# Moving a finished chunk's split and logits, and the next batch's key chunk, to other places in the order of an attention and mixture-of-experts kernel

## The chip, the cores and the metric

The kernel runs on one core of a Trainium2 chip, as one program and one launch. The metric is the time on the device in microseconds (us): the median of three runs, 1411.36 us, with 1410.93 and 1411.73 as the lowest and the highest.

## What is computed

Two steps follow each other. The first is an attention without softmax over 8 batches of 2496 rows: scores of z with itself, squared after a ReLU, times v, and the result times u. The second sends each of the 19968 rows to one of 8 experts and computes an expert's two-layer network for its 80 rows of highest gate weight alone; all other rows of the output are zero.

```python
def _attn_ref(u, v, z):
    scale = 1.0 / S
    scores = scale * np.matmul(z, z.transpose(0, 2, 1))
    attn = np.maximum(scores, 0.0) ** 2
    out = np.matmul(attn, v)
    return u * out

def _moe_ref(x, w_gate, w1, w2, capacity):
    logits = x @ w_gate
    expert_idx = np.argmax(logits, axis=1)
    ...
    for e in range(E):
        ...
            keep = np.argpartition(-gw, capacity)[:capacity]
        h = np.maximum(x[tok_idx] @ w1[e], 0.0)
        out[tok_idx] = gate_w[tok_idx, None] * (h @ w2[e])
```

## The kernel before, in words

The 2496 rows of a batch are padded to 20 tiles of 128. Queries are taken in 5 chunks of 4 tiles (the last chunk has 448 columns, not 512), keys in 10 pairs of tiles. A step is one (batch b, chunk qc, pair r); the 400 steps are one list, and the loop over it writes out the order of each engine's work by hand: under `manual_schedule` PE, ACT, DVE and SP run their instructions in the order in which the loop issues them. Each of these engines takes its instructions strictly one after the other, so an instruction that waits holds everything behind it.

A step has two sides. `scores` (line 312) prepares a pair that is used two steps later (`LOOK` is 2). For a pair not yet seen PE makes two score tiles `s` (lines 326, 327, two matmuls each), ACT applies ReLU and square (lines 330, 331), and the result `a` is split into a rounded part `ah` (a cast on ACT or DVE, lines 105 and 107) and the remainder `al` (a subtraction on DVE, line 54). Since the scores are symmetric, pairs of key chunks before qc are not computed again: DVE transposes them when they are first made (`mirror`, line 265), a DMA stores them to DRAM (`y`), another reads them back (`blk`), and `mirrored` (line 299) casts `ah` on ACT (line 310) and subtracts `al` on DVE. `attend` (line 341) is then PE's main work: for each of the two key tiles and two halves of the output three matmuls of 512 columns, v's rounded part with `ah`, its remainder with `ah`, and its rounded part with `al` (lines 358 to 360; lines 362 and 363 for the padded last tile). The pools bound how far the engines can be apart: three `s` tiles, two `a`, three `ah` and three `al`.

When a chunk's ten pairs are done, its result is finished during the next chunk's steps:

- `chunk_x` (line 380): DVE multiplies the accumulated tile by u into `xf`, two instructions at line 377, at the start of the next chunk's step r = 0, ahead of that step's `scores`.
- `chunk_hi`, `chunk_rest`, `chunk_mid`, `chunk_lo` (lines 386 to 400): x is split into three bf16 parts. ACT casts `xb<-xf` (line 388), DVE subtracts `xr` (line 54), ACT casts `xb<-xr` (line 396), DVE subtracts the third part.
- `chunk_store`, `chunk_store2`: SP issues two DMA transposes of `xf` (line 427) and a store (line 436).
- `chunk_logits`, `chunk_sum`: 24 small matmuls on PE (line 451) and a reduction on DVE (line 459) give the gate logits.

`finished` (line 714) says at which step r of the next chunk each of these is issued; `at_end` is the last batch's fourth chunk, which has steps of its own, with `gate_top` and `gate_near` (DVE work on the batch's logits, with one ACT exponential at line 483). The loop itself is at lines 770 to 822. The fourth chunk of a batch starts with the pairs 8 and 9 and goes on with 0 to 7.

The next batch's keys are loaded one chunk of 512 columns at a time: SP issues `load_z` (line 100) at r = 1, and `prep_zc` (line 109) splits it on DVE in two instructions (a cast at line 112 and a subtraction at line 54, together `zc`) at r = 9.

After the last batch, DVE and PE finish the last chunk's x and logits, rows are picked, gathered and sent through the experts' matmuls.

Of the kernel before, what the change touches and what calls it, by code (L numbers as in the profile page):

```python
# [25 lines left out]
def attn_moe_kernel(ctx, tc, zT, uT, v, wg, w1, w2, out, seq, cap):  # L26
# [341 lines left out]
    def chunk_tiles(b, qc):  # L368
        xf = xpool.tile([P, DC, CH], F32, tag="xf", name=f"xf_{b}_{qc}")

        xb = xpool.tile([P, 3, DC, CH], BF16, tag="xb", name=f"xb_{b}_{qc}")
        xr = xpool.tile([P, DC, CH], F32, tag="xr", name=f"xr_{b}_{qc}")
        nq = min(CH, seq - qc * CH)
        xt_t[b, qc] = [x[..., :nq] for x in (xf, xb, xr)]

    def x_full(b, qc, c, s):
        V.scalar_tensor_tensor(out=xt_t[b, qc][0][:, c, s], in0=acc_t[b, qc][c][:, s], scalar=CSQ,  # L377
                               in1=u_t[b, qc][:, c, s], op0=ALU.mult, op1=ALU.mult)

    def chunk_x(b, qc):  # L380
        s = slice(0, min(CH, seq - qc * CH))
        chunk_tiles(b, qc)
        for c in range(DC):
            x_full(b, qc, c, s)

    def chunk_hi(b, qc):
        xf, xb, _ = xt_t[b, qc]
        nc.scalar.copy(out=xb[:, 0], in_=xf)  # L388

    def chunk_rest(b, qc):  # L390
        xf, xb, xr = xt_t[b, qc]
        tt(xr, xf, xb[:, 0], ALU.subtract)

    def chunk_mid(b, qc):
        _, xb, xr = xt_t[b, qc]
        nc.scalar.copy(out=xb[:, 1], in_=xr)  # L396
# [317 lines left out]
    def finished(b, qc, r):  # L714

        at_end = b == B - 1 and qc == NQ - 2
        if r == 0:
            chunk_hi(b, qc)
        elif r == 1:
            chunk_rest(b, qc)  # L720
        if r == (3 if at_end else 1):
            chunk_store(b, qc)
        if r == (5 if at_end else 3):
            chunk_store2(b, qc)
        if r == 1 and at_end or r == 2 and not at_end:
            chunk_mid(b, qc)
        if r == (2 if at_end else 3):
            chunk_lo(b, qc)
        if r == (4 if at_end else 6):
            chunk_logits(b, qc)  # L730
            chunk_sum(b, qc)
        kb = b * BPB
        if b < B - 1 and qc == NQ - 1:
            if r == 7:
                gate_top(b, 0, NQ)
            elif r == 8:
                gate_sum(b, gate_near(b, 0), gp)
        elif qc == 0 and b > 0:
            part = kb - BPB, kb
            if r == 2:  # L740
                count(*part)
            elif r == 4:
                up_to(*part)
                blocks(ps_m, "m", gp, oh, *part)
        elif at_end:
            part = kb, kb + BPB - 2
            if r == 5:
                gate_top(b, 0, NQ - 1)
            elif r == 6:
                gate_near(b, 0)  # L750
            elif r == 8:
                count(*part)
                up_to(*part)
                half()
            elif r == 9:
                blocks(ps_m, "m", gp, oh, *part)

    with tc.manual_schedule(engines={ET.PE, ET.Activation, ET.DVE, ET.SP}):
        prep_zc(0, 0, raw0)
        prep_zd(0, 0, raw0)  # L760
        prep_v(0, 0, vraw0, V, V)
        prep_zc(0, 1, raw12[:, 0])
        scores(0, 0, 0)
        scores(0, 0, 2)
        warm(WARM0, ps_m, "m")
        v_raw[0, 1] = vraw1
        z_raw.update({(0, 2): raw12[:, 1], (0, 3): raw34[:, 0], (0, 4): raw34[:, 1]})
        constants()
        prev = None
        for i, (b, qc, r) in enumerate(steps):  # L770
            last = b == B - 1 and qc == NQ - 1
            now[0] = i
            if r == 0 and prev:
                chunk_x(*prev)
            if (b, qc) == (0, 0) and r in (0, 2, 4):
                prep_zc(0, r // 2 + 2, z_raw.pop((0, r // 2 + 2)))
            if i + LOOK < len(steps):
                nb, nqc, nr = steps[i + LOOK]
                scores(nb, nqc, 2 * pairs_of[nqc][nr])
            if b == 0 and qc == 0:  # L780
                if r % 2 == 0 and r < 8:
                    g = r // 2 + 1
                    prep_v(0, g, v_raw.pop((0, g)), nc.scalar, V)
                    if g + 1 < NQ:
                        v_raw[0, g + 1] = load_v(0, g + 1)
                if r == 8:
                    constants_v()
            p = pairs_of[qc][r]
            for k in (2 * p, 2 * p + 1):
                if not last or k < NT - 3:  # L790
                    attend(b, qc, k)
            if prev:
                finished(*prev, r)

            nb, nqc = (b, qc + 1) if qc + 1 < NQ else (b + 1, 0)
            if r == 2:
                prep_u(b, qc)
            if b + 1 < B:
                if r == 1:
                    z_raw[b + 1, qc] = load_z(b + 1, qc)  # L800
                if r == 9:
                    prep_zc(b + 1, qc, z_raw.pop((b + 1, qc)))
                if qc == NQ - 2 and r in (2, 4):
                    g = r // 2 - 1
                    v_raw[b + 1, g] = load_v(b + 1, g)
                if qc == NQ - 1:
                    g = (r - 1) // 2 if r < 9 else 4
                    if r in (2, 4, 6, 8, 9):
                        prep_v(b + 1, g, v_raw.pop((b + 1, g)), nc.scalar, V)
                        if g + 2 < NQ:  # L810
                            v_raw[b + 1, g + 2] = load_v(b + 1, g + 2)
            if nb < B and r == 1:
                prep_zd(nb, nqc)
            if r == 5 and b < B - 1:
                zero_out(b * NQ + qc, B * NQ)
            if r == 8 and b == 0:
                zero_out((B - 1) * NQ + qc, B * NQ)
            if b == B - 1 and qc >= NQ - 3:
                weights_ahead(qc, r)
            mirror_back()  # L820
            mirror_out()
            if r == NP - 1:
                prev = b, qc

        chunk_tiles(*prev)
        for kk, c in ((3, 0), (2, 0), (3, 1), (1, 0), (2, 1), (1, 1)):
            attend(*prev, NT - kk, [c])
            if kk == 1:
                chunk_x_last(*prev, c)
        chunk_store(*prev)  # L830
        chunk_logits_last(*prev)
        gate_top(b, NQ - 1, NQ)
        chunk_store2(*prev)
        kb = B * BPB
        count_last(kb - 2, kb)
        blocks(ps_s, "s", gp, oh, kb - 2, kb)
        ranks()
# [562 lines left out]
```

## Time and profile before

| what | value |
|---|---|
| median of 3 runs | 1411.36 us |
| lowest to highest | 1410.93 to 1411.73 us |
| the profiled execution | 1410.26 us |
| its span, first to last instruction | 1408.5 us |
| PE (matmuls) busy | 1373.3 us, 97% |
| PE's weight loads busy | 1139.7 us, 81% |
| DVE busy | 1063.8 us, 76% |
| ACT busy | 1002.6 us, 71% |
| POOL busy | 35.4 us, 3% |
| DMA queues, share of 16 engines | 79.6% and 0.4% |

The page tells of one profiled execution. The span runs from its first instruction to its last. The busy time of an engine is the time in which it has an instruction in work; the busy shares are means over stages that differ: seven batches that are alike, a last batch, and some 90 us of expert work behind it. In a timeline each row is one instruction (or several alike in a row, marked x2, x8) with its start and its length in us; brackets give the idle time of the engine just before it and what ended that idle time. A matmul's length is longer than its distance from the next, since matmuls overlap in the array; the distance of two starts tells the pace.

### The profile page before, as it was taken

The page shows a single profiled execution, that of the slowest core. Times are in us where ns is not written, and L with a number is a line of the kernel's source. Part 1 is how long each engine was busy: PE and PEld are TensorE (multiplying, and loading weights), DVE is VectorE, ACT ScalarE, POOL GpSimd, SP SyncE. Part 2 cuts the span into 40 slices and gives each one's busy share as a digit, 9 for nine tenths or more (in the row PEclk, how much of TensorE's full clock was granted, in tenths as well). Part 3 has the DMA queues.
Part 4 walks back from the last instruction along what each step waited for, and adds up shares of the span by engine and source line. Part 5 has one row for each costly group of instructions (what it writes and reads, how often), then busy time and mean ns, then how long its engine had stood idle before and what let it go on. Part 6 is the DMA issues. An engine that isn't in the chain of part 4 may idle for free. (4 is left out here: it accounts for less than half of the span.)

```text
span 1408.5 us, 19544 instructions
## 1 busy us (share of the span) xinstructions
PE 1373.3 (97%) x7086; PEld 1139.7 (81%) x7087; DVE 1063.8 (76%) x1517; ACT 1002.6 (71%) x1282; POOL 35.4 (3%) x56
## 2 busy tenths in 40 slices
PE   9999999999999999999999999999999999999777
PEld 7887888888887888878888888878888788888566
DVE  8876788667877678767886678776886678867864
ACT  8875777757777587757787577766877577876365
POOL 0000000000000000000000000000000000000152
PEclk9999999999999999999999999999999999999889
DMA  6899777995888966996789958889668967889673
GB/s 223 254 254 264 207 220 225 246 264 156 227 231 236 265 176 197 253 260 172 221 232 246 255 166 232 228 231 259 175 204 249 262 168 202 239 222 244 170 231 93
DMA packets 260070, 311.89 MB, mean 221 GB/s; under 512 B 96152, under 2 KB 188192, under 8 KB 249728
## 3 DMA queue, kind: packets, MB, share of 16 engines
q1 hardware_dynamic: 258752, 309.02, 79.6%
q0 software_dynamic: 1216, 1.56, 0.4%
q8 instruction: 57, 0.93, 0.3%
q14 instruction: 45, 0.37, 0.1%
HBM read 153.48 MB, written 126.37 MB: 199 GB/s over the span
## 5 line engine op out<-in xcount | busy, mean ns | idle before, releaser
L360 PE MATMUL acc<-al,vt 128*128 128x512 f32 (+1 forms) x1520 | 585.5, 385 | 8.3 <-DVE al L54 8.3
L359 PE MATMUL acc<-ah,vt 128*128 128x512 f32 (+1 forms) x1520 | 584.7, 385 | 0.0
L358 PE MATMUL acc<-ah,vt 128*128 128x512 f32 (+1 forms) x1520 | 584.4, 384 | 0.0
L54 DVE TENSOR_TENSOR al<-a,ah 128x1024 fp32r<-128x1024 f32 (+1 forms) x240 | 291.4, 1214 | 136.1 <-ACT ah L105 128.4
L330 ACT ACTIVATE a<-s 128x512 f32<-128x512 f32 (+1 forms) x480 | 258.3, 590 | 129.6 <-PE s L327 128.4
L360 PEld LDWEIGHTS acc<-al,vt 128*128 128x128 f32 x1520 | 285.3, 188 | 64.1 <-DVE al L54 12.3
L359 PEld LDWEIGHTS acc<-ah,vt 128*128 128x128 f32 x1520 | 285.2, 188 | 53.7 <-DVE vt L146 0.8
L358 PEld LDWEIGHTS acc<-ah,vt 128*128 128x128 f32 x1520 | 285.4, 188 | 52.9
L331 ACT ACTIVATE a<-a 128x1024 f32<-128x1024 f32 (+1 forms) x240 | 253.0, 1054 | 7.6
L54 DVE TENSOR_TENSOR al<-blk,ah 128x1024 fp32r<-128x1024 f32 x160 | 193.7, 1216 | 42.9 <-ACT ah L310 40.7
L310 ACT CAST ah<-blk 128x1024 fp32r<-128x1024 f32 x160 | 165.4, 1048 | 76.9 <-PE acc L359 54.9
L265 DVE STREAM_TRANSPOSE x<-a 128x512 f32<-128x512 f32 x320 | 207.6, 687 | 0.0
L327 PE MATMUL s<-zd,zc 128*128 128x512 f32 (+1 forms) x480 | 186.9, 389 | 0.0
L105 ACT CAST ah<-a 128x1024 fp32r<-128x1024 f32 x153 | 160.8, 1051 | 4.8
L107 DVE CAST ah<-a 128x1024 fp32r<-128x1024 f32 (+1 forms) x87 | 59.2, 680 | 111.1 <-ACT a L331 111.0
L326 PE MATMUL s<-zc,zc 128*128 128x512 f32 x320 | 128.8, 403 | 1.7 <-ACT a L330 1.7
L327 PEld LDWEIGHTS s<-zd,zc 128*128 128x128 f32 x480 | 90.4, 188 | 16.2 <-issue 0.5
L388 ACT CAST xb<-xf 128x1024 bf16<-128x1024 f32 (+1 forms) x39 | 40.1, 1028 | 83.4 <-DVE xf L377 83.4
L326 PEld LDWEIGHTS s<-zc,zc 128*128 128x128 f32 x320 | 60.1, 188 | 15.2 <-ACT a L330 4.3
L326 PE MATMUL s<-zc 128*128 128x512 f32 (+1 forms) x160 | 63.6, 397 | 0.0
L396 ACT CAST xb<-xr 128x1024 bf16<-128x1024 f32 (+1 forms) x39 | 40.0, 1024 | 28.2 <-DVE xr L54 27.7
L146 DVE TENSOR_TENSOR vt<-vraw,vt 128x1024 fp32r<-128x1024 f32 (+1 forms) x40 | 46.5, 1163 | 6.8 <-ACT vt L105 6.5
(171 smaller groups left out, 841.9 us busy)
## 6 DMA issues: line engine op xcount, KB each, us to landing
y<-x SPq DMA_DIRECT2D x80, 1024.0 KB
blk<-y SPq DMA_DIRECT2D x320, 256.0 KB
out<-idle SPq DMA_DIRECT2D x40, 512.0 KB
vraw<-v SPq DMA_DIRECT2D x32, 512.0 KB
ut<-uT SPq DMA_DIRECT2D x32, 512.0 KB
xs<-xq SPq DMA_DIRECT2D x32, 512.0 KB
wraw<-w SPq DMA_DIRECT2D x28, 512.0 KB
zd<-zc SPq DMA_DIRECT2D x78, 128.0 KB
```

Source lines behind the costliest of these rows:

```text
L54: V.tensor_tensor(out=o, in0=a, in1=b, op=op)
L105: eng.copy(out=o, in_=i)
L107: eng.tensor_copy(out=o, in_=i)
L265: V.transpose(out=x[:, :, :, t].rearrange("p n k s -> p k n s"), in_=a)
L310: nc.scalar.copy(out=natural(ah), in_=src)
L326: nc.tensor.matmul(s[:, :nq], zk, zc[:, :nq], start=True, stop=False)
L327: nc.tensor.matmul(s[:, :nq], zk, zd[:, :nq], start=False, stop=True)
L330: nc.scalar.activation(out=a[:, h, :nq], in_=s[:, :nq], func=AF.Relu)
L331: nc.scalar.activation(out=a[:, :, :nq], in_=a[:, :, :nq], func=AF.Square)
L358: nc.tensor.matmul(o, vt[:, t, 0, cs], ah, start=k == first, stop=False)
L359: nc.tensor.matmul(o, vt[:, t, 1, cs], ah, start=False, stop=False)
L360: nc.tensor.matmul(o, vt[:, t, 0, cs], al, start=False, stop=k == last)
```

## The change

Three things move, and nothing is added or removed.

1. `chunk_x` is issued behind step r = 0's `scores`, not ahead of it. Since the order on DVE is the order of issue, the remainder `al` of the pair that is used two steps later now stands ahead of the two x instructions.
2. `finished` issues the parts of the split a step later: `chunk_hi` at r = 1 for 0, `chunk_rest` at 2 for 1, `chunk_mid` at 3 for 2, `chunk_lo` at 4 for 3 (in the last batch's fourth chunk `chunk_mid` at 2 for 1, `chunk_lo` at 3 for 2). The store's steps stay. The logits stay at r = 6, and in the last batch's fourth chunk move from r = 4 to r = 5, with `gate_top` from 5 to 6 and `gate_near` from 6 to 7.
3. `prep_zc` for the next batch is issued at r = 5, not r = 9. Its load stays at r = 1.

```diff
@@ -714,19 +714,19 @@
     def finished(b, qc, r):
 
         at_end = b == B - 1 and qc == NQ - 2
-        if r == 0:
+        if r == 1:
             chunk_hi(b, qc)
-        elif r == 1:
+        elif r == 2:
             chunk_rest(b, qc)
         if r == (3 if at_end else 1):
             chunk_store(b, qc)
         if r == (5 if at_end else 3):
             chunk_store2(b, qc)
-        if r == 1 and at_end or r == 2 and not at_end:
+        if r == (2 if at_end else 3):
             chunk_mid(b, qc)
-        if r == (2 if at_end else 3):
+        if r == (3 if at_end else 4):
             chunk_lo(b, qc)
-        if r == (4 if at_end else 6):
+        if r == (5 if at_end else 6):
             chunk_logits(b, qc)
             chunk_sum(b, qc)
         kb = b * BPB
@@ -744,9 +744,9 @@
                 blocks(ps_m, "m", gp, oh, *part)
         elif at_end:
             part = kb, kb + BPB - 2
-            if r == 5:
+            if r == 6:
                 gate_top(b, 0, NQ - 1)
-            elif r == 6:
+            elif r == 7:
                 gate_near(b, 0)
             elif r == 8:
                 count(*part)
@@ -770,13 +770,13 @@
         for i, (b, qc, r) in enumerate(steps):
             last = b == B - 1 and qc == NQ - 1
             now[0] = i
-            if r == 0 and prev:
-                chunk_x(*prev)
             if (b, qc) == (0, 0) and r in (0, 2, 4):
                 prep_zc(0, r // 2 + 2, z_raw.pop((0, r // 2 + 2)))
             if i + LOOK < len(steps):
                 nb, nqc, nr = steps[i + LOOK]
                 scores(nb, nqc, 2 * pairs_of[nqc][nr])
+            if r == 0 and prev:
+                chunk_x(*prev)
             if b == 0 and qc == 0:
                 if r % 2 == 0 and r < 8:
                     g = r // 2 + 1
@@ -798,7 +798,7 @@
             if b + 1 < B:
                 if r == 1:
                     z_raw[b + 1, qc] = load_z(b + 1, qc)
-                if r == 9:
+                if r == 5:
                     prep_zc(b + 1, qc, z_raw.pop((b + 1, qc)))
                 if qc == NQ - 2 and r in (2, 4):
                     g = r // 2 - 1
```

How the rows stand on the engines, at three places. In these names the first numbers are the chunk and the key tile or part, the last one counts buffers.

DVE, batch 1, start of the fourth chunk (`al_3_0` is the remainder of the pair used at r = 2, `xf_2` the third chunk's x), before:

```order
L112 CAST zc_2_2729<-zraw_2469 128x512
L54 TENSOR_TENSOR zc_2_2729<-zraw_2469,zc_2_2729 64x512
L377 SCALAR_TENSOR_TENSOR xf_2_2744<-acc_2_0_2429,ut_2_2501 128x512
L377 SCALAR_TENSOR_TENSOR xf_2_2744<-acc_2_1_2430,ut_2_2501 128x512
L54 TENSOR_TENSOR al_3_0_2751<-blk_3_0_2396,ah_3_0_2749 128x1024
L54 TENSOR_TENSOR al_3_2_2770<-blk_3_0_2396,ah_3_2_2768 128x1024
L54 TENSOR_TENSOR xr_2_2746<-xf_2_2744,xb_2_2745 128x1024
```

and with the change:

```order
L54 TENSOR_TENSOR al_3_0_2746<-blk_3_0_2399,ah_3_0_2744 128x1024
L377 SCALAR_TENSOR_TENSOR xf_2_2748<-acc_2_0_2429,ut_2_2500 128x512
L377 SCALAR_TENSOR_TENSOR xf_2_2748<-acc_2_1_2430,ut_2_2500 128x512
L54 TENSOR_TENSOR al_3_2_2769<-blk_3_0_2399,ah_3_2_2767 128x1024
L54 TENSOR_TENSOR al_3_4_2799<-blk_3_1_2443,ah_3_4_2797 128x1024
L54 TENSOR_TENSOR xr_2_2750<-xf_2_2748,xb_2_2749 128x1024
```

The two `zc` rows are gone from here (they stand after the third chunk's `al_2_14` now), `al_3_0` stands ahead of the two `xf` rows, and `xr_2` one pair later.

ACT, batch 1, start of the second chunk (`xb_0` is the first part of the first chunk's x, `s_1_6` and `s_1_7` the score tiles of the pair used at r = 3), before:

```order
L388 CAST xb_0_2078<-xf_0_2077 128x1024
L330 ACTIVATE a_1_6_2111<-s_1_6_2112 128x512
L330 ACTIVATE a_1_6_2111<-s_1_7_2115 128x512
L331 ACTIVATE a_1_6_2111<-a_1_6_2111 128x1024
L330 ACTIVATE a_1_8_2146<-s_1_8_2147 128x512
L330 ACTIVATE a_1_8_2146<-s_1_9_2150 128x512
```

and with the change:

```order
L330 ACTIVATE a_1_6_2110<-s_1_6_2111 128x512
L330 ACTIVATE a_1_6_2110<-s_1_7_2114 128x512
L331 ACTIVATE a_1_6_2110<-a_1_6_2110 128x1024
L388 CAST xb_0_2092<-xf_0_2091 128x1024
L330 ACTIVATE a_1_8_2145<-s_1_8_2146 128x512
L330 ACTIVATE a_1_8_2145<-s_1_9_2149 128x512
```

The cast of x, which reads what DVE has just made, stands behind the two ReLUs and the square of a pair, not ahead of them.

DVE, last batch, last chunk (`mx_0` to `oh` are `gate_top`, `fw_0` and `ex_last` are `gate_near`, `w2l` a split of an expert's weights), before:

```order
L54 TENSOR_TENSOR al_4_14_12434<-blk_4_3_12178,ah_4_14_12432 128x1024
L478 TENSOR_REDUCE mx_0_12449<-lg_11640 128x16
L54 TENSOR_TENSOR d_0_12451<-lg_11640,mx_0_12449 128x128
L486 SCALAR_TENSOR_TENSOR fw_0_12454<-d_0_12451,first_w 128x128
L489 TENSOR_REDUCE mf_0_12456<-fw_0_12454 128x16
L490 TENSOR_TENSOR oh<-fw_0_12454,mf_0_12456 128x8x2x8
L107 CAST ah_4_16_12469<-a_4_16_12459 128x2x448
L54 TENSOR_TENSOR al_4_16_12471<-a_4_16_12459,ah_4_16_12469 128x2x448
L505 TENSOR_SCALAR fw_0_12454,nsum<-d_0_12451 128x128
L507 SCALAR_TENSOR_TENSOR ex_last<-ex_last,fw_0_12454 128x128
```

and with the change:

```order
L54 TENSOR_TENSOR al_4_14_12408<-blk_4_3_12178,ah_4_14_12406 128x1024
L459 TENSOR_REDUCE lg_11640<-pl_3_12423 128x32
L107 CAST ah_4_16_12459<-a_4_16_12449 128x2x448
L54 TENSOR_TENSOR al_4_16_12461<-a_4_16_12449,ah_4_16_12459 128x2x448
L478 TENSOR_REDUCE mx_0_12475<-lg_11640 128x16
L54 TENSOR_TENSOR d_0_12477<-lg_11640,mx_0_12475 128x128
L486 SCALAR_TENSOR_TENSOR fw_0_12480<-d_0_12477,first_w 128x128
L489 TENSOR_REDUCE mf_0_12482<-fw_0_12480 128x16
L490 TENSOR_TENSOR oh<-fw_0_12480,mf_0_12482 128x8x2x8
L625 TENSOR_TENSOR w2l_60_12486<-wraw_2_0_12361,w2h_59_12485 128x1024
L107 CAST ah_4_18_12499<-a_4_18_12489 128x2x448
L54 TENSOR_TENSOR al_4_18_12501<-a_4_18_12489,ah_4_18_12499 128x2x448
```

`gate_top`'s five rows stand behind `al_4_16`, no longer ahead of it, and `gate_near`'s two behind `al_4_18`. POOL's and SP's rows stand in the same order as before.

## Rows read from the trace of the kernel before

**Rows 1.** The page: busy time of PE and others; granted PE clock by fortieths of the span.

```profile
PE 1373.3 (97%) x7086; PEld 1139.7 (81%) x7087; DVE 1063.8 (76%) x1517; ACT 1002.6 (71%) x1282; POOL 35.4 (3%) x56
PEclk9999999999999999999999999999999999999889
```

**Rows 2.** Waits of PE: line, released by; us in total, times, longest.

```profile
PE acc L360 <- DVE al L54: 8.3, 8, 1.2
...
PE s L326 <- ACT a L330: 1.7, 6, 0.3
```

**Rows 3.** Timeline of PE, batch 1, fourth chunk: start, length, engine, line, what.

```profile
282.57 0.39 PE L358 MATMUL acc<-ah,vt 128*128 128x512 f32 x1
282.79 0.39 PE L359 MATMUL acc<-ah,vt 128*128 128x512 f32 x1
284.33 0.50 PE L360 MATMUL acc<-al,vt 128*128 128x512 f32 x1 [1.15 <-DVE al L54]
284.67 0.40 PE L358 MATMUL acc<-ah,vt 128*128 128x512 f32 x1
```

**Rows 4.** Timeline of DVE, the same place.

```profile
279.50 1.30 DVE L265 STREAM_TRANSPOSE x<-a 128x512 f32<-128x512 f32 x2
280.72 0.39 DVE L112 CAST zc<-zraw 128x512 fp32r<-128x512 f32 x1
281.14 0.69 DVE L54 TENSOR_TENSOR zc<-zraw,zc 64x512 fp32r<-64x512 f32 x1
281.86 1.29 DVE L377 SCALAR_TENSOR_TENSOR xf<-acc,ut 128x512 f32<-128x512 f32 x2
283.06 1.21 DVE L54 TENSOR_TENSOR al<-blk,ah 128x1024 fp32r<-128x1024 f32 x1
```

**Rows 5.** Timeline of ACT, the same place.

```profile
278.23 1.04 ACT L310 CAST ah<-blk 128x1024 fp32r<-128x1024 f32 x1
283.18 1.05 ACT L388 CAST xb<-xf 128x1024 bf16<-128x1024 f32 x1 [3.91 <-DVE xf L377]
```

**Rows 6.** Timeline of PE, batch 1, second chunk, its first steps.

```profile
210.91 0.39 PE L327 MATMUL s<-zd,zc 128*128 128x512 f32 x1
...
214.54 0.39 PE L327 MATMUL s<-zd,zc 128*128 128x512 f32 x1
215.22 0.50 PE L326 MATMUL s<-zc,zc 128*128 128x512 f32 x1 [0.29 <-ACT a L330]
215.55 0.40 PE L327 MATMUL s<-zd,zc 128*128 128x512 f32 x1
```

**Rows 7.** Timeline of ACT, the same place.

```profile
213.62 1.05 ACT L388 CAST xb<-xf 128x1024 bf16<-128x1024 f32 x1 [3.73 <-DVE xf L377]
214.57 1.08 ACT L330 ACTIVATE a<-s 128x512 f32<-128x512 f32 x2
```

**Rows 8.** Timeline of PE, last batch, fourth chunk.

```profile
1270.38 0.50 PE L360 MATMUL acc<-al,vt 128*128 128x512 f32 x1 [0.27 <-DVE al L54]
```

**Rows 9.** Timeline of DVE, last batch, end of the last chunk.

```profile
1307.86 0.28 DVE L478 TENSOR_REDUCE mx<-lg 128x16 f32<-128x128 f32 x1
...
1309.14 0.29 DVE L490 TENSOR_TENSOR oh<-fw,mf 128x128 bf16<-128x128 f32 x1
1310.70 0.63 DVE L107 CAST ah<-a 128x896 fp32r<-128x896 f32 x1 [1.26 <-ACT a L331]
...
1318.72 1.28 DVE L377 SCALAR_TENSOR_TENSOR xf<-acc,ut 128x256 f32<-128x256 f32 x4
```

**Rows 10.** Timeline of SP, batch 1, third chunk, second pair: the key load.

```profile
255.29 0.57 SPq L100 DMA_DIRECT2D zraw<-zT  x1
```

**Rows 11.** Timeline of DVE, batch 1, third chunk, behind the sixth pair's work.

```profile
266.76 1.22 DVE L54 TENSOR_TENSOR al<-a,ah 128x1024 fp32r<-128x1024 f32 x1 [1.19 <-ACT ah L105]
```

**Rows 12.** Timeline of SP, last batch: the last of a block's four loads.

```profile
1291.09 0.30 SPq L292 DMA_DIRECT2D blk<-y  x1
```

**Rows 13.** Timeline of ACT, last batch: the cast that waits for that block.

```profile
1302.14 1.05 ACT L310 CAST ah<-blk 128x1024 fp32r<-128x1024 f32 x1 [0.53 <-DMA blk<-y]
```

## The prediction

> **What bounds the kernel.** I read the page first. PE is busy for 97% of the span, no other engine for more than 76%, and its granted clock stands at the full level, 2.4 GHz, until the last slices [rows 1]. So the question is what PE lacks to 100%, and where. PE's pace is read from starts: in the attention loop a matmul of 512 columns starts 0.22 to 0.23 us after the one before (282.57, 282.79) [rows 3], and I count 0.227 per matmul. Time can only come from places where the distance is longer, or be lost by making new ones.
>
> The list of PE's waits names them. Inside the attention loop only two groups count: 8 waits of a matmul at line 360 for an `al` of DVE, 8.3 us in all, and 6 waits of a score matmul at line 326 for ACT's ReLU, 1.7 us in all [rows 2]. The first kind lies at the start of a fourth chunk: in batch 1 the matmul at 284.33 sat idle for 1.15 us [rows 3]; seven such and the 0.27 us of the last batch [rows 8] make 8.3. The second lies in the second step of a second chunk, 0.29 us each [rows 6].
>
> The Trainium skill's page "Perfetto Trace Analysis", section "Identifying the Most-Contended Engine", calls a matmul's busy share a poor measure and judges headroom by the weight loads' share. That share is 81% [rows 1], so by the page a fifth of the span, some 270 us, would be open; an estimate. The trace does not bear it out as headroom, since the distance of starts is even between the waits.
>
> **The fourth chunk's wait.** Its cost is more than the idle time shown. 282.79 to 284.33 is 1.54 us, and 284.33 to 284.67 is 0.34, where 0.227 each is the pace [rows 3]: 1.31 and 0.11 too long, together 1.42 us. Seven times that is 9.9 us. For the last batch I take double its idle time, 0.5 us.
>
> Why it waits: DVE runs the two transposes to 280.72, then the `zc` pair (280.72 to 281.86), then x (281.86 to 283.06), and only then the `al` that PE lacks, 283.06 to 284.27 [rows 4]. No row of these has an idle time before it. `ah`, which `al` reads, was there at 278.23 + 1.04 = 279.27 [rows 5]. So the wait is DVE's queue alone. With the change `zc` is gone from here and `al` stands in front: it runs from 280.72 to about 281.93. PE wants it at 282.79 + 0.23 = 283.02, so 1.1 us are to spare. x follows at 281.86, the very time at which it starts now, so the transposes that SP issues from it come no later.
>
> What is late next? The following pair's `al` stands behind x, at 283.06 as the present one does, and ends at 284.27, if ACT has its `ah`. ACT now sits idle for 3.91 us ahead of the cast of x [rows 5]; with that cast behind it, the pair's `ah` is no longer held by it. PE wants this `al` twelve matmuls after the first one, 283.02 + 12 x 0.227 = 285.7: 1.5 us to spare.
>
> **The second chunk's wait.** PE's score matmul waits at 215.22, 0.68 us after the matmul before, and the next follows at 0.33 [rows 6]: 0.45 and 0.10 over the pace, 0.56 us, six times 3.4 us. It waits for one of the three score tiles, whose reader is ACT's ReLU at 214.57. That ReLU stands behind the cast of x, and ACT sat idle for 3.73 us ahead of the cast, until DVE had x [rows 7], while the scores were there at 210.91 + 0.39 = 211.3 [rows 6]. With the change the ReLU stands first and can start at 211.3, over 3 us sooner; the cast takes its 1.05 us behind it, where ACT has those idle microseconds.
>
> **The key chunk.** `zc` costs DVE 281.86 - 280.72 = 1.14 us wherever it stands [rows 4], 35 times (five chunks of seven batches). At its new place DVE now sits idle for 1.19 us [rows 11], so there it costs nothing. If that cover were gone, its 1.14 us would stand ahead of an `al` that is used two steps later. Its load must land sooner: it is issued at 255.29 [rows 10] and read at about 265.6, 10.3 us later, where it has until 280.72 today. How long such a load takes no row shows. The nearest one from above is a block's last load: issued at 1291.09 [rows 12], with ACT waiting for it until 1302.14 [rows 13], 11.05 us; from below, nothing beyond its issue, 0.57 us. I take it as landed in time, since the block is four loads at once and this is one.
>
> **The split's parts, and the logits.** The same instructions stand a step later, that is 2.7 us of PE work (12 attention matmuls at 0.227) or 3.6 (with four score matmuls), each where its engine has its idle time. Only the logits on PE wait for them: the third part is now made two steps before the logits, not three. In the last batch's fourth chunk the two are two steps apart before and after, and the waits list has no wait at line 451 there, so I cost it at nothing.
>
> **The end of the loop.** This is where something is lost. Behind 1310.70 DVE stands idle no more until the last chunk's x at 1318.72 [rows 9], and all that follows hangs on that x. `gate_top`, 1307.86 to 1309.14 + 0.29, 1.57 us, stands ahead of that stretch now; with the change it stands inside. Against it the idle 1.26 us, which wait for ACT [rows 9], can fall away. So the loss lies between nothing and 1.6 us, plus the 0.5 us that PE gains in the fourth chunk and cannot keep if DVE is last: at most 2.1. I take 1.2, above the middle, since the pair behind `gate_top` waits in turn for the exponential on ACT, plus 0.3 for one new short wait in the last chunk, of the size of today's [rows 8].
>
> **The sum.** 9.9 + 0.5 + 3.4 - 1.2 - 0.3 = 12.3 us gained. The profiled execution took 1410.26 us, 1.1 under the median of 1411.36; from it 1398.0 us, from the median 1399.1, which I give.
>
> **Rivals.** *The wait moves one pair on* (A). If DVE or ACT reaches the next pair late instead, half of the gain goes: some 6 us, 1405. For it speaks that DVE's total work is unchanged; against it the 1.5 us to spare worked out above, and that an idle time stands within a few rows.
>
> *Buffers bind, not order* (B). A repeated gap of equal size can come from a tile that isn't free: three `al`, three score tiles. Then moving rows gives nothing, 1411. For the second chunk's wait the row itself is one for a free tile, but its reader is late by the queue [rows 7], and at the fourth chunk DVE's rows follow each other without idle time [rows 4]. The Trainium skill's page "Perfetto Trace Analysis", section "Optimization Strategy", says that the same gap repeating can mean too little SBUF or PSUM for the next tile. By that rule the time would stay at 1411; the trace agrees for the tile, not for the cause.
>
> *The key load comes late* (C), the side on which it gets slower. DVE is held by the cast that reads it, with every `al` behind it. Up to 1 us late is hidden by the pair's two steps of lead; beyond that, which is 11.4 us from the issue, each microsecond costs PE one at each of 35 loads. At 11.4 + 12.3 / 35 = 11.75 us the gain is eaten; at 12.2 us the kernel would take 1411 - 12 + 28 = 1427. For it speaks the 11.05 us above, against it that the block is four times the bytes, and that SP is held by the key load's issue for just 0.57 us [rows 10].
>
> *It doesn't do what it says* (D): the rows of the order say that it does; 1411.
>
> **Chances.** Forecast 0.85, A 0.06, B 0.04, C 0.04, D 0.01. Range: the best of the forecast keeps the whole 13.8 us and fills the 1.26 us of idle time at the end besides, 1396.3; the worst leaves the second chunk's waits as they are and loses the full 2.1 + 0.3 at the end, 1411.4 - 9.9 - 0.5 + 2.4 = 1403.4, taken up to 1404.5 to reach towards A. Left out are B, C, D and half of A, 0.12, and what of the forecast's own case I may have overlooked. A difference under 0.2%, 2.8 us, can't be told from none here. So faster 0.91 (forecast and A), within 0.2% 0.05 (B, D), slower 0.04 (C).
>
> **What would show it.** In the changed kernel's list of PE's waits both groups of rows 2 should be gone or below 1 us; DVE's `al` at the fourth chunk's start should run straight behind the transposes, with x behind it; ACT's idle time ahead of the cast of x should be below 1 us, with the ReLUs in front; no `zc` cast should wait for a DMA; the last chunk's x should start 0.5 to 2 us after PE's last attention matmul could hand over. The forecast is wrong if PE waits at line 360 one pair further on, if line 451 appears among the waits, or if the loop's end comes 12 us sooner but the kernel's end does not.

## The result, and the profile after

The changed kernel took 1397.89 us (median of five executions, 1396.17 to 1401.54), the kernel before 1411.36. The ratio is 0.9907 with a 95% interval of 0.9892 to 0.9922: 0.9% faster, by about 13 us. The forecast was 1399.1 us in a range of 1396.3 to 1404.5. In two later series, on two chips, the changed kernel took 1398.06 and 1398.55 us (both below), where the kernel before took 1410.42 and 1410.65: 12.4 and 12.1 us less.

The list of PE's waits in the changed kernel, to be held against [rows 2]:

```profile
PE fp L662 <- DVE few L58: 5.6, 1, 5.6
...
PE pl L416 <- DVE xf L377: 1.2, 1, 1.2
```

Both groups of [rows 2] are gone. What is left lies in the expert part, but for 1.4 us at the kernel's start, 0.3 us at line 359 in the first batch, and the new line 416, the first logits of the very last chunk, which wait for its x.

The start of batch 1's fourth chunk, on PE, DVE and ACT of the changed kernel, answers to [rows 3 to 5]:

```profile
280.68 0.39 PE L358 MATMUL acc<-ah,vt 128*128 128x512 f32 x1
280.90 0.39 PE L359 MATMUL acc<-ah,vt 128*128 128x512 f32 x1
281.13 0.39 PE L360 MATMUL acc<-al,vt 128*128 128x512 f32 x1
```

```profile
277.61 1.30 DVE L265 STREAM_TRANSPOSE x<-a 128x512 f32<-128x512 f32 x2
278.83 1.18 DVE L54 TENSOR_TENSOR al<-blk,ah 128x1024 fp32r<-128x1024 f32 x1
279.93 1.28 DVE L377 SCALAR_TENSOR_TENSOR xf<-acc,ut 128x512 f32<-128x512 f32 x2
281.13 1.21 DVE L54 TENSOR_TENSOR al<-blk,ah 128x1024 fp32r<-128x1024 f32 x1
```

```profile
278.38 1.05 ACT L310 CAST ah<-blk 128x1024 fp32r<-128x1024 f32 x1 [1.00 <-PE acc L359]
281.25 1.05 ACT L388 CAST xb<-xf 128x1024 bf16<-128x1024 f32 x1 [1.81 <-DVE xf L377]
```

PE keeps its 0.227 us across the place where a start came 1.54 us after the one before. `al` ends at 278.83 + 1.18 = 280.01 and PE reads it at 281.13: 1.12 us to spare, where the forecast had 1.1. ACT still sits idle for 1.81 us ahead of the cast of x, but nothing that PE lacks stands behind it now.

The second chunk's second step, PE of the changed kernel, answers to [rows 6]; then ACT, to [rows 7]:

```profile
213.26 0.39 PE L327 MATMUL s<-zd,zc 128*128 128x512 f32 x1
213.49 0.39 PE L326 MATMUL s<-zc,zc 128*128 128x512 f32 x1
213.71 0.39 PE L327 MATMUL s<-zd,zc 128*128 128x512 f32 x1
```

```profile
210.55 0.60 ACT L330 ACTIVATE a<-s 128x512 f32<-128x512 f32 x1
211.18 1.06 ACT L331 ACTIVATE a<-a 128x1024 f32<-128x1024 f32 x1
213.09 1.05 ACT L388 CAST xb<-xf 128x1024 bf16<-128x1024 f32 x1 [0.84 <-DVE xf L377]
```

The ReLU and the square now stand ahead of the cast, and the score matmul comes at the pace.

The loop's end: PE, then DVE, of the changed kernel; DVE answers to [rows 9]. Then a row of PE and one of DVE of the kernel before.

```profile
1304.76 0.37 PE L363 MATMUL acc<-al,vt 128*128 128x448 f32 x1
1306.34 1.95 PE L416 MATMUL pl<-wg_sb,xf 128*128 128x8 f32 x16 [1.18 <-DVE xf L377]
```

```profile
1304.72 1.22 DVE L625 TENSOR_TENSOR w2l<-wraw,w2h 128x1024 fp32r<-128x1024 f32 x1
1305.86 1.28 DVE L377 SCALAR_TENSOR_TENSOR xf<-acc,ut 128x256 f32<-128x256 f32 x4
1308.33 0.19 DVE L478 TENSOR_REDUCE mx<-pl 128x4 f32<-128x32 f32 x1 [1.19 <-PE pl L416]
```

```profile
1318.76 0.37 PE L363 MATMUL acc<-al,vt 128*128 128x448 f32 x1
```

```profile
1321.18 0.19 DVE L478 TENSOR_REDUCE mx<-pl 128x4 f32<-128x32 f32 x1 [1.18 <-PE pl L416]
```

The last attention matmul (line 363) starts at 1304.76; before, it started at 1318.76. So the loop ends 14.0 us sooner. But DVE has `gate_top` among its last rows now, with idle times of 0.35 and 0.63 us behind it, and comes to x at 1305.86 only, behind a weight's split; PE waits 1.18 us for it. From line 363 to the last chunk's logits maximum (line 478) it takes 3.57 us where it took 2.42: 1.15 us of the 14.0 are given back, which leaves 12.85.

The rest of the span is the expert part, and its length differs between executions. From that maximum to the span's end it is 87.4 us before, 91.4 in this profiled execution (1401.54 us, the longest of the five), 86.9 and 88.1 in the profiled executions of the two later series. Windows of 94.9 and 91.7 us behind line 363, in this execution and in the second of those (columns: window, its length, busy times of PE, its weight loads, DVE, ACT and POOL with their counts, granted clock, DMA share, GB/s):

```profile
1304.80:1399.70 94.90, 66.85 (x415) 52.21 (x414) 58.33 (x176) 46.83 (x82) 34.96 (x37) 0.83 0.48 149
```

```profile
1304.80:1396.50 91.70, 68.31 (x415) 52.64 (x414) 58.29 (x176) 46.75 (x82) 34.56 (x37) 0.82 0.50 155
```

The same kernel, the same work and nearly the same clock, 3.2 us apart: this difference is not a matter of the change. From here on I compare where line 363 starts for the loop and the medians for the whole.

### The profile page after: what moved, and what is told of

Read it like the earlier page. It is cut to its first block, busy times and chain, and to the rows that moved or that the text cites. A ratio compares the mean times of both kernels' runs of the same rounds, so it can differ in the third digit from the quotient of the medians.

```text
span 1399.7 us, 19558 instructions
## 1 busy us (share of the span) xinstructions
PE 1369.4 (98%) x7086; PEld 1141.5 (82%) x7087; DVE 1060.5 (76%) x1517; ACT 1009.3 (72%) x1282; POOL 37.0 (3%) x56
## 4 chain that ended last, share of the span: by engine, by line
PE 91%; DVE 3%; ACT 2%; DMA 2%; issue 1%; POOL 0%; POOLq 0%; SPq 0%; DVEq 0%; ACTq 0%
PE acc L360 23%; PE acc L359 23%; PE acc L358 23%; PE s L326 8%; PE s L327 7%; PE op L1189 2%; PE pl L451 2%; PE acc L362 1%; PE acc L363 1%; PE hp L1159 1%; DMA blk<-y 1%; DMA xs<-xq 1%; DVE al L54 1%; ACT a L331 1%; ACT a L330 1%
## 5 line engine op out<-in xcount | busy, mean ns | idle before, releaser
L377 DVE SCALAR_TENSOR_TENSOR xf<-acc,ut 128x512 f32<-128x512 f32 (+2 forms) x82 | 50.1, 652 | 0.0
```

## The experiments

The change has three parts: x behind the first pair's scores (X), x's parts a pair later (P), the key chunk at the sixth pair (Z). The later logits and gate of the last batch's fourth chunk belong to it too: the kernels with two of the parts, made from the changed one, have them, and the kernels with one part, made from the one before, have not. The theory was the forecast's: two waits, each made by the order on one engine. The rivals were that one part does nearly all, that the parts depend on each other, and that the gain is bounded by buffers or by the key load. Six kernels take the parts singly and in pairs.

**Z alone**, on the kernel before:

```diff
-                if r == 9:
+                if r == 5:
                     prep_zc(b + 1, qc, z_raw.pop((b + 1, qc)))
```

> The kernel before with the key chunk's split alone moved from the tenth pair to the sixth. Theory (the fourth chunk's wait is the amount of DVE work ahead of the remainder, whichever it is): without the 1.14 us of the split the remainder ends at 283.1 where PE wants it at 283.02, so the seven waits of 1.15 us fall to 0.1 or 0.2 each; x comes 1.14 us sooner in the second chunk too, which is more than its 0.29 us of idle time, so those six go as well. Time 1398 to 1401, nearly the whole gain from this part alone. Rival (each part brings its own share, and x behind the scores is the main one): the waits at line 360 stay above 0.7 us each, 1405 or more.

Measured: 1399.87 us (1398.31 to 1402.6), ratio 0.9924 (0.9908 to 0.9939). Both groups of [rows 2] are gone, line 363 starts at 1307.13: 11.6 of the loop's 14.0 us come with this one line. It also cures the second chunk's wait, which the forecast had put down to ACT's order alone. ACT in batch 1's second chunk with Z alone, to be held against [rows 7]:

```profile
211.63 1.05 ACT L388 CAST xb<-xf 128x1024 bf16<-128x1024 f32 x1 [2.55 <-DVE xf L377]
```

With no `zc` ahead of it x is there sooner: ACT stands 2.55 us ahead of the cast where it stood 3.73, and so the cast that holds the ReLU is over sooner.

**X and P without Z**, the changed kernel with the key chunk back at r = 9 (the diff above, turned round):

> The changed kernel with the key chunk's split back at the tenth pair. Theory (two cures of one wait, each nearly enough alone): the remainder stands ahead of x but behind the split, 281.86 to 283.07, so PE waits 0.1 or 0.2 us at a fourth chunk; in the second chunk a remainder now stands behind the split with x behind it, a few tenths there. Time 1398 to 1402. Rival (the shares add up): the split's 1.14 us comes back seven times, 8 us, so 1406.

Measured: 1399.57 us (1399.37 to 1401.61), ratio 0.9923 (0.9909 to 0.9938), line 363 at 1307.0. So X and P together cure the same waits a second time: two nearly complete cures, whose gains don't add.

**P alone**, on the kernel before, and **P and Z**, the changed kernel with x in front again:

```diff
-        if r == 0:
+        if r == 1:
             chunk_hi(b, qc)
-        elif r == 1:
+        elif r == 2:
             chunk_rest(b, qc)
...
-        if r == 1 and at_end or r == 2 and not at_end:
+        if r == (2 if at_end else 3):
             chunk_mid(b, qc)
-        if r == (2 if at_end else 3):
+        if r == (3 if at_end else 4):
             chunk_lo(b, qc)
```

```diff
+            if r == 0 and prev:
+                chunk_x(*prev)
             if (b, qc) == (0, 0) and r in (0, 2, 4):
...
                 scores(nb, nqc, 2 * pairs_of[nqc][nr])
-            if r == 0 and prev:
-                chunk_x(*prev)
```

> The kernel before with one part of the change alone: the finished chunk's parts a pair later (the last batch's logits and gate stay where they were). Theory (two waits with two causes): the wait of L326 for ACT goes (3.4 us), the wait of L360 for DVE at the fourth chunks stays at 1.2 us in 6 or 7 places, since the key chunk and x still stand ahead of that subtraction: 1406 to 1408 us. Rival (the waits are one pile-up at the chunk's start, and any one of the three moves empties it, as the key chunk's move alone did): both waits gone, 1399 to 1401 us.

> The changed kernel with the finished chunk's x put back in front of the first pair's scores; the parts stay a pair later and the key chunk stays at the sixth pair. Theory (the fourth chunk's wait came from the key chunk and x both standing ahead of one subtraction on DVE, and either one taken away cures it; the second chunk's wait came from the first part and is cured by the parts' move): no wait of L360 or L326 of over 0.15 us, the last attention matmul starts within 1305 to 1307 us, 1398 to 1400 us. Rival (x's own move is needed with the parts where they are now): a wait of L360 or L326 for DVE at every chunk's start, 39 times 0.1 to 0.5 us, 1402 to 1418 us.

Measured: P alone 1409.27 us (1407.11 to 1410.96), ratio 0.9987 (0.9977 to 0.9996), line 363 at 1316.0. P and Z 1399.74 us (1398.69 to 1400.64), ratio 0.9926 (0.9909 to 0.9942), line 363 at 1307.0. PE's waits with P alone:

```profile
PE acc L360 <- DVE al L54: 8.1, 7, 1.2
...
PE pl L451 <- DVE xb L54: 1.6, 1, 1.6
```

The fourth chunk's wait stays and the second chunk's is gone, as the theory of two causes has it. The loop gains 2.8 us, the whole 1.4 against the 1410.65 us of the kernel before on the same chip, less than expected. The new line 451 is one reason: P alone leaves the logits of the last batch's fourth chunk at r = 4, only one pair behind x's third part, and they wait for it. By the distances of starts that costs 1.7 us, against 3.4 gained at the second chunks and 0.7 in the last batch's fourth chunk; the remaining 0.4 are spread over the loop. Behind Z, P adds nothing (1307.1 and 1307.0), there with the logits moved too.

**X alone**, and **X and Z with the parts put back**:

```diff
-            if r == 0 and prev:
-                chunk_x(*prev)
             if (b, qc) == (0, 0) and r in (0, 2, 4):
...
                 scores(nb, nqc, 2 * pairs_of[nqc][nr])
+            if r == 0 and prev:
+                chunk_x(*prev)
```

> The kernel before with one part of the change alone: the finished chunk's x behind the first pair's scores; the parts stay at the first pairs and the key chunk at the tenth. Theory (x behind the scores pushes DVE's and ACT's part work into the step in which the next pair's exponentials are due, so x's move needs the parts' move): waits of L326 for ACT of 14 to 39 times 1 to 1.5 us as in the run with the parts put back, a little fewer where the key chunk was the cause there, 1425 to 1437 us. Rival (in that run it was the key chunk at the sixth pair that met the parts, and x alone is harmless): under 1412 us, and the fourth chunk's wait of L360 gone.

> The changed kernel with the four parts of the split of x back at their steps of before (0, 1, 2, 3; in the last batch's fourth chunk 0, 1, 1, 2), x itself behind the scores as changed. Theory (ACT's order makes the second chunk's wait, and the parts had to follow x): the cast of x on ACT stands ahead of the next pair's ReLUs again while x comes later on DVE by the remainder ahead of it, so ACT is held at the start of every chunk, by 1.2 us more in the second and up to 2.5 in the first; PE's waits at line 326 come back larger than the 0.29 us of before and at first chunks too, and the time is above that of the kernel before: 1415 to 1440. Rival (the parts' step does not matter, since their engines have idle time): 1397 to 1400.

Measured: X alone 1455.14 us (1453.64 to 1456.18), ratio 1.032 (1.0303 to 1.0338); X and Z 1433.67 (1432.38 to 1434.33), ratio 1.0158 (1.0139 to 1.0176). PE's waits with X alone, then PE and ACT at the second chunk of batch 1:

```profile
PE s L326 <- ACT a L330: 26.4, 15, 2.3
...
PE acc L358 <- ACT ah L310: 5.1, 8, 0.7
PE acc L360 <- DVE al L54: 5.0, 9, 0.7
```

```profile
218.09 0.39 PE L327 MATMUL s<-zd,zc 128*128 128x512 f32 x1
220.72 0.50 PE L326 MATMUL s<-zc,zc 128*128 128x512 f32 x1 [2.24 <-ACT a L330]
```

```profile
219.12 1.04 ACT L388 CAST xb<-xf 128x1024 bf16<-128x1024 f32 x1 [5.68 <-DVE xf L377]
220.08 1.08 ACT L330 ACTIVATE a<-s 128x512 f32<-128x512 f32 x2
```

Here is what the parts' move is for. With the cast of x still issued at r = 0, ACT stands in front of it for 5.68 us until DVE has made x (217.81 to 219.09, now behind an `al`); the next pair's ReLU is queued behind the cast, and PE waits 2.24 us for the score tile. The same picture as [rows 7], at 5.68 for 3.73 us. That X alone is harmless is refuted; its cost was underestimated by 18 us. Six waits of line 326 were 2.23 to 2.26 us, not 1 to 1.5, and behind four of these six PE's granted clock fell to 0.50, that is 1.2 GHz, for 3.4 us (from 390.8, 561.5, 899.4 and 1070.1), in which matmuls start 0.43 us apart; that is some 6 of the 42 us, an estimate from these distances. (The "exponentials" of the expectation are the ReLU and the square of lines 330 and 331.)

The eight cases side by side; line 363's start in the profiled execution, and the median:

| parts | line 363, us | median, us |
|---|---|---|
| none | 1318.8 | 1411.36 |
| P | 1316.0 | 1409.27 |
| Z | 1307.1 | 1399.87 |
| P, Z | 1307.0 | 1399.74 |
| X, P | 1307.0 | 1399.57 |
| X, P, Z | 1304.8 | 1397.89 |
| X, Z | 1340.7 | 1433.67 |
| X | 1361.0 | 1455.14 |

Z alone leaves the last batch's gate where it was, and so does not pay at the loop's end: the last chunk's maximum stands at 1309.57 with it, at 1308.33 in the changed kernel, at 1321.18 before. By that mark one line brings 11.6 of the 12.85 us, and X and P bring 10.6 without it (1310.58): the rival that one part does nearly all holds for Z, which is nearly enough and yet not needed. The ratios' intervals of Z alone and of the changed kernel overlap (0.9908 to 0.9939, 0.9892 to 0.9922), so their medians alone do not tell them apart.

**Where the last 2.2 us are.** Three kernels end the loop at 1307.0 or 1307.1 with at most 0.3 us of waits at lines 360 and 326 in PE's list, the changed one at 1304.8. The start of batch 1's fourth chunk in the kernel with X and P, PE and then DVE:

```profile
281.43 0.39 PE L359 MATMUL acc<-ah,vt 128*128 128x512 f32 x1
281.78 0.50 PE L360 MATMUL acc<-al,vt 128*128 128x512 f32 x1
282.11 0.40 PE L358 MATMUL acc<-ah,vt 128*128 128x512 f32 x1
```

```profile
279.77 0.69 DVE L54 TENSOR_TENSOR zc<-zraw,zc 64x512 fp32r<-64x512 f32 x1
280.49 1.23 DVE L54 TENSOR_TENSOR al<-blk,ah 128x1024 fp32r<-128x1024 f32 x1
```

`al` ends at 281.72 and PE's matmul starts at 281.78, 0.35 us after the one before, and the next 0.33 after that: 0.12 and 0.10 over the pace, with no idle time in brackets, since the earlier matmul is still in the array. Seven fourth chunks (the last batch prepares no keys) make 1.5 of the 2.2 us; some 0.3 lie in the first 40 us of the span, and the rest I did not place. With Z alone or with P and Z it is x, not `zc`, that stands ahead of the `al`, and the rows read alike. What waits for `al` is the matmul's weight load; the same place with X and P, then in the changed kernel:

```profile
281.77 0.19 PEld L360 LDWEIGHTS acc<-al,vt 128*128 128x128 f32 x1 [0.38 <-DVE al L54]
```

```profile
280.91 0.19 PEld L360 LDWEIGHTS acc<-al,vt 128*128 128x128 f32 x1
```

The page shows it over the whole kernel (last column: idle time before the loads, and how much of it `al` ended); X and P first, the changed kernel's execution in the last series second:

```profile
L360 PEld LDWEIGHTS acc<-al,vt 128*128 128x128 f32 x1520 | 285.3, 188 | 56.0 <-DVE al L54 4.4
```

```profile
L360 PEld LDWEIGHTS acc<-al,vt 128*128 128x128 f32 x1520 | 285.4, 188 | 52.9 <-DVE al L54 1.2
```

**The loop's end.** Two ways to have the 1.15 us back. One puts the last batch's logits and gate where they were (r = 4, 5, 6); the other keeps the change and holds one subtraction of the weights' split back until the last x is issued:

```diff
-        if r == (5 if at_end else 6):
+        if r == (4 if at_end else 6):
             chunk_logits(b, qc)
...
-            if r == 6:
+            if r == 5:
                 gate_top(b, 0, NQ - 1)
-            elif r == 7:
+            elif r == 6:
                 gate_near(b, 0)
```

> The changed kernel with the last batch's fourth chunk as before in its logits and its gates (logits at the fifth pair, gates at the sixth and seventh), the parts of x as changed, so the third part is one step ahead of the logits. Theory (the 1.18 us that PE waits for the last x come from the gate work that now stands in DVE's last busy stretch): that wait goes; against it PE waits at line 451 for the third part, 0.5 to 2 us. Time within 1 us of the changed kernel. Rival (the last x is late by the weight split just ahead of it, whatever the gates do): the 1.18 us stay and the wait at line 451 adds, 1 to 2 us slower.

Measured: 1397.51 us (1397.35 to 1398.81), ratio 0.9906 (0.989 to 0.9921). The wait at line 416 is gone, and line 363 to the maximum is 2.22 us; but the logits at r = 4 come before their third part is there, and line 363 starts at 1306.0, 1.2 us later:

```profile
PE pl L451 <- DVE xb L54: 1.6, 1, 1.6
```

So the logits' move by one pair is paid for by what it gives: the maximum stands at 1308.20 here and at 1308.33 in the changed kernel, and the medians are 0.4 us apart, with intervals that overlap. That the wait at line 416 is gone is in part PE's own delay: x starts at 1305.56, only 0.3 us sooner. But counted from the last of the score matmuls for the last chunk's ninth pair (line 327, at 1294.95 here and at 1293.27 in the changed kernel) DVE comes to x after 10.6 us here and after 12.6 there, so the gate's place does make x late.

```diff
+        if hold:
+            held.append((lv[:, s], rv, hv[:, s]))
+            return
...
+        for o, i0, i1 in held:
+            tt(o, i0, i1, ALU.subtract)
         chunk_store(*prev)
         chunk_logits_last(*prev)
```

> The changed kernel, with the subtraction of one weight split on DVE (1.22 us, just ahead of the last chunk's x) issued behind that x. Theory (DVE's queue is last at the loop's end, and sits idle for 1.18 us behind x while PE makes the logits): PE's wait at line 416, 1.18 us, goes, and the subtraction fills the idle time; 1 us faster than the changed kernel, 1396 to 1397.5. Rival (the subtraction then stands ahead of the maximum that all that follows waits for): no gain, the same time.

> The changed kernel once more, beside the three that follow. Its profiled execution lay 3.6 us above its median, the one of before 1.1 below its own. Theory (the loop is the same in each execution, the expert part is not): PE's last attention matmul starts at 1304.8 again to within 0.3 us, and the time behind it differs by some us. Rival (the loop itself varies): the last attention matmul starts at another time, by the same amount as the whole.

Measured side by side on one chip: with the subtraction held back 1396.52 us (1396.0 to 1397.84), ratio 0.9895 (0.9878 to 0.9912); the changed kernel again 1398.06 (1397.14 to 1398.59), ratio 0.9903 (0.9886 to 0.992), line 363 at 1305.2 (and 4.51 us from there to the maximum, since the sixteen small matmuls of line 416 took 2.90 us in that execution, not 1.95, with a granted clock of 0.57 from 1307 to 1311). PE of the first at the loop's end:

```profile
1305.52 1.95 PE L416 MATMUL pl<-wg_sb,xf 128*128 128x8 f32 x16 [0.19 <-DVE xf L377]
```

The wait falls from 1.18 to 0.19 us, and line 363 to the maximum from 3.57 to 2.57. Its median is the lowest of all kernels run; but the two intervals overlap, so the 1.0 us is shown by the rows and not by the medians. A second step goes for PE's longest wait in the expert part, line 662: the flag that says whether a general path has to run is made three experts later:

```diff
-                if i == 3:
+                if i == 6:
                     last_flags()
```

> The kernel with the subtraction behind x, and the flag's matmul (line 662), for which PE stands 5.6 us in the expert part, issued three experts later. Theory (PE's queue sets the end of the expert part): 2 to 5 us faster, 1392 to 1395. Rival (DVE's splits and the weights' loads pace it, PE's wait is where it would wait anyway): within 1 us of the kernel without this.

Measured: 1396.96 us (1396.69 to 1397.1), ratio 0.9896 (0.988 to 0.9913): nothing gained over the kernel it was added to, where 2 to 5 us were expected. PE's wait for the flag is 4.5 us, where it was 5.1 without this step.

**The key load.** The changed kernel with the load issued one step before its use, at r = 4:

```diff
-                if r == 1:
+                if r == 4:
                     z_raw[b + 1, qc] = load_z(b + 1, qc)
```

> The changed kernel with the key chunk's load issued at the fifth pair, one step ahead of the split that reads it at the sixth, not four. It measures how long such a load takes, by DVE's idle time ahead of line 112. Theory (one load of 128 x 512 takes 4 to 6 us under this traffic): issued some 3 us ahead of the split, it holds DVE for 1 to 3 us per chunk, part of which the pair's lead hides; 1400 to 1440. Rival (it takes the 11 us of the block's load): DVE is held by 7 us or more at each of 35, 1550 or more. If it takes under 3 us, nothing is held: 1398.

Measured: 1469.04 us (1466.5 to 1475.06), ratio 1.0402 (1.0382 to 1.0421), line 363 at 1380.7. Waits of DVE and of PE, then SP and DVE around the first long wait, and PE's windows there:

```profile
DVE zc L112 <- DMA zraw<-zT: 111.4, 14, 15.8
```

```profile
PE acc L358 <- DVE ah L107: 55.2, 7, 9.3
```

```profile
128.97 6.64 SPq L292 DMA_DIRECT2D blk<-y  x4
135.65 0.73 SPq L100 DMA_DIRECT2D zraw<-zT  x1
```

```profile
145.23 0.43 DVE L112 CAST zc<-zraw 128x512 fp32r<-128x512 f32 x1 [15.83 <-DMA zraw<-zT]
```

```profile
171.81 0.43 DVE L112 CAST zc<-zraw 128x512 fp32r<-128x512 f32 x1 [0.58 <-DMA zraw<-zT]
```

```profile
131.00:137.00 6.00, 6.00 (x49) 4.90 (x48) 0.00 (x0) 3.71 (x6) 0.00 (x0) 1.00 1.07 374
137.00:143.00 6.00, 0.90 (x4) 0.40 (x3) 0.00 (x0) 1.04 (x1) 0.00 (x0) 0.99 1.07 232
143.00:149.00 6.00, 1.73 (x3) 1.00 (x4) 3.60 (x6) 0.00 (x0) 0.00 (x0) 0.50 1.09 280
149.00:155.00 6.00, 6.00 (x19) 4.72 (x18) 3.75 (x4) 1.05 (x1) 0.00 (x0) 0.66 0.37 112
```

One of the 14 waits (3.7 us) is the kernel's first load, as before; so 13 of 35 loads come late, and not alike. Seven, one in each batch's fourth chunk, hold DVE for 13.6 to 15.8 us: the first of them stood on SP behind four `blk` loads that held SP for 6.64 us, was issued at 135.65 only, and was read 9.6 us after that, in a stretch with a DMA share of 1.07 and more. The next one, issued at 167.04, was read after 4.8 us, with DVE waiting 0.58 us for it. At the six such places, all in fifth chunks, it is 4.8 to 7.0 us. So the long waits are SP's queue and a slower landing together; which share each has was not tried. In and behind the 9.3 us in which PE had nothing its granted clock was at 0.50, that is 1.2 GHz, and at 0.66 in the next window, which is one reason why the loop's end comes 75.9 us later for 55.2 us of waits.

**A third execution of the changed kernel**, beside the kernels with x in front, P alone and X alone:

> The changed kernel itself, as a mark for the three runs beside it on the same chip. Theory: 1397 to 1399 us, the last attention matmul starts at 1304.8 us within 0.5, as in its other two traces, and what differs between executions lies in the expert part behind it. Rival: the last attention matmul moves by over 1 us between chips.

Measured: 1398.55 us (1397.66 to 1398.99), ratio 0.9916 (0.99 to 0.9933), line 363 at 1304.8. Over the three profiled executions of this kernel that start is 1304.8, 1305.2 and 1304.8; from it to the span's end it is 94.9, 91.5 and 91.7 us.

A fourth buffer for `al` or for the score tiles was not tried. The order alone removed the waits, with every pool as it was; whether a buffer more would have done so too is open.

## Why the prediction was right, and where it was not

**The fourth chunk's wait** (9.9 and 0.5 us): right in its cause and its size. DVE's rows follow each other as forecast, with 1.12 us to spare for 1.1, and the forecast's loop gain of 13.5 us (9.9 + 0.5 + 3.4 - 0.3) stands against 14.0. By the distances of starts before and after, the seven fourth chunks give 9.9 and the six second chunks 3.4, as forecast; the last batch's fourth chunk gives 0.9.

**The 1.1 us to spare**: this number explains the table. Leave `zc` (1.14 us) or x (1.2 us) ahead of the `al`, and all of it is used up; 0.22 us per place remains. It is that much, and not 0.02, because the forecast counted to the matmul: what waits is its weight load, which starts 0.22 us before it (280.91 and 281.13), so 0.90 us are to spare. The forecast said that both go, and did not ask what either does alone. It would have found that Z alone takes 1.14 us out of the row that was 1.31 too late, and so nearly all.

**The second chunk's wait** (3.4 us): gone, but only one of its two causes was named. ACT's order was the one given; Z alone also removed it. P alone removed it too, and gave 2.8 us in the loop, after the 1.7 it lost at the last batch's logits.

**The parts cost nothing** (the step that was wrong in its reasoning, though not in its sum): they were costed as a move between idle times. They are the condition on which X is of use at all: without P the loop's end comes 36 to 42 us later (1340.7 for 1304.8, 1361.0 for 1318.8). The forecast's sum for the whole change does not contain this, because it took all parts as made. That the last batch's logits stay two steps behind the parts it did reckon with; P alone and the kernel with the end put back show the price where they don't, 1.6 us at line 451.

**The key chunk at nothing, the load in time**: right. In the changed kernel the shortest time from a load's issue to its cast is 7.2 us (151.19 to 158.37), with no idle time ahead of the cast, and a load that DVE waited for took 4.8 to 7.0 where it was not issued behind a block's. The forecast had no row for such a load and argued from a block's four, so how near it came was not known. Rival C did not come; but its form, one equal delay at each of 35 loads, was wrong: the run with the late load shows 13, seven of them long, by SP's queue and a slower landing.

**The end** (1.2 us): 1.15 measured, in the place forecast, through `gate_top` inside DVE's last busy stretch. The 1.2 was a choice between nothing and 2.1, so it is in part luck that the figure came out. The 0.3 for one new short wait: two starts at line 360 in the last chunk come late, at 1289.82 and 1302.59, 0.46 and 0.50 us after the matmul before where 0.20 is the pace, 0.56 together, and 0.76 with the start behind each (0.31). They are too short for the list of waits.

**The sum**: 12.3 forecast, 14.0 - 1.15 = 12.85 in the traces, 1411.36 - 1397.89 = 13.47 between the medians, 12.4 and 12.1 in the later series. Rivals A, B and D fell with the empty list of waits. For B the Trainium skill's page "Perfetto Trace Analysis", section "Optimization Strategy", says that a gap repeating on the engine to be kept full can mean too little SBUF or PSUM for the next tile; the runs here don't bear it out for this gap, which a change of order alone took away (11.6 us with one line), with every pool as it was. One of the forecast's signs, ACT idle for less than 1 us ahead of the cast of x, was met in the second chunk (0.84) and not in the fourth (1.81), without cost.

## What to carry to other kernels

Where a wait is made by several instructions standing ahead of the one that is needed, taking away any of them may cure it: work out the time to spare first, and see which single move exceeds it, before counting the moves' gains together. When a producer is moved back in one engine's queue, move every consumer that waits for it in other engines' queues too; here the producer's move alone cost 42 us at the loop's end because a cast that waits for it stood ahead of PE's next ReLU. And a matmul can be late without idle time on PE: read the distance of starts, or the weight load's row.

## What the runs showed of the hardware

A matmul that starts 0.1 us late shows in no wait list of PE: the matmul before is still in the array (0.39 us long at a pace of 0.227), and only the distance of starts and the weight load's idle time tell (4.4 against 1.2 us). PE's granted clock stayed at the full level behind the seven waits of 1.15 us of the kernel before; behind six waits of 2.23 to 2.26 us, with X alone, it fell to 0.50 four times, for 3.4 us each, and stayed at full level twice (behind 220.72 and 730.34); in and behind the wait of 9.3 us it was at 0.50 too. And when a DMA's data can be read hung on where it was issued, too: a key load that was read 4.8 to 7.0 us after its issue at six places held DVE for 13.6 to 15.8 us at seven others, the first of which stood on SP behind four loads that held it for 6.64 us.
